# Reordering the backward pass of an SSM-gated FFN block: convolution backward first, parameter sums spread over two stages, w1/w3 gradient copies moved to ScalarE, part of w1/w3 transposed early

## The chip, the cores and the metric

The kernel runs on one core of a Trainium2 chip. The metric is the device time of one execution in microseconds (us), lower is better. Times are medians of a few executions; executions of one kernel differ by up to 1%, so runs on the same chip beside the kernel before are compared by ratios.

## The reference, cut to what matters

The forward function is a layer norm, a state-space convolution `s` (length 2048, 576 channels, 128 states), and a gate `silu(FFN(xn))` with hidden width 4608. The kernel computes the forward result and the gradients of all inputs.

```python
def _B_ref(x, w1, w3, w2):
    gate = jnp.einsum("bsd,df->bsf", x, w1)
    up = jnp.einsum("bsd,df->bsf", x, w3)
    h = _silu(gate) * up
    return jnp.einsum("bsf,fd->bsd", h, w2)

x = A_u
xn = _layernorm(x, axis=-1)
s = _A_ref(xn, A_re, A_im, B_re, B_im, C_re, C_im, log_dt, Dskip)   # FFT convolution
g = _silu(_B_ref(xn, w1, w3, w2))
return x + s * g
# reference(): this value and its vjp with grad_out, for every input
```

The backward half has four kinds of work that matter here: the FFN weight gradients (18 groups of 256 hidden columns), the backward of the convolution (four quarters of the channels), the sums for the SSM parameters (36 chunks of 16 channels, then one "final parameter step"), and the FFN input gradients (16 tiles of 128 rows).

Of the kernel before, what the change touches and what calls it, by code (L numbers as in the profile page):

```python
# [11 lines left out]
ALU = mybir.AluOpType  # L12
# [48 lines left out]
class K:  # L61
# [393 lines left out]
    def kgen_chunk(self, ch, E, lhs, SEL, mp, sb, sb1, ps, ps1):  # L455
# [27 lines left out]
        nc.gpsimd.tensor_scalar(out=pz[:, :, :, 0].rearrange("p g h d a -> p (g h) (d a)"),  # L483
# [202 lines left out]
    def ffn_hidden(self, wp, gup, ps, T0, TA):  # L686
# [4 lines left out]
        NT = 2  # L691
        nfull = D // P
# [3 lines left out]
        for fb in range(F // FB):  # L696
# [9 lines left out]
            for i0 in range(0, LT, NT):  # L706
                self.at(T0 + TA * 4 * fb + TA * 4 * i0 // LT)
                g_t = gup.tile([P, NT, FB], BF16, name="g_t")
                u_t = gup.tile([P, NT, FB], BF16, name="u_t")
                s_t = gup.tile([P, NT, FB], BF16, name="s_t")  # L710
                h_t = gup.tile([P, NT, FB], BF16, name="h_t")
                for q in range(NT):
# [8 lines left out]
                    nc.scalar.activation(out=s_t[:, q, :], in_=pg[:], func=ACT.Silu)  # L721
                    if q % 2 == 0:
                        nc.vector.tensor_copy(out=g_t[:, q, :], in_=pg[:])
                    else:
                        nc.scalar.copy(out=g_t[:, q, :], in_=pg[:])  # L725
                    nc.scalar.copy(out=u_t[:, q, :], in_=pu[:])
                nc.vector.tensor_tensor(out=h_t[:], in0=s_t[:], in1=u_t[:], op=ALU.mult)
                nc.sync.dma_start(out=self.H_dram[i0:i0 + NT, :, f0:f0 + FB].rearrange("t p f -> p t f"), in_=h_t[:])
                for k in range(FB // self.FG):
                    gs = slice(k * self.FG, (k + 1) * self.FG)  # L730
                    for (dst, src) in ((self.G_dram, g_t), (self.U_dram, u_t)):
                        nc.gpsimd.dma_start(out=dst[fb * (FB // self.FG) + k, :, i0:i0 + NT, :], in_=src[:, :, gs])  # L732
# [71 lines left out]
    def phase5_ssm_bwd(self, T0, TQ):  # L804
        nc, cfg = self.nc, self.cfg
        D, LT, N = cfg.D, cfg.LT, cfg.N
        Wq = D // 4
        with self.tc.tile_pool(name="b_fix", bufs=1) as fix, \
                self.tc.tile_pool(name="b_ps", bufs=3, space=bass.MemoryType.PSUM) as ps:
            S_all = fix.tile([P, 4, D], FP32, name="S_all")  # L810
            self.lcol = fix.tile([P, LT], FP32, name="lcol")
# [3 lines left out]
            self.ones_col = fix.tile([P, 1], BF16, name="ones_col")  # L815
            nc.vector.memset(self.ones_col[:], 1.0)
            self.dskip_row = fix.tile([P, D], BF16, name="dskip_row")
# [5 lines left out]
            for g in range(4):  # L823
                with self.tc.tile_pool(name="b_gk", bufs=1) as gkp:
                    gK = gkp.tile([P, 2, 2, LT, Wq // 2], BF16, name="gK")
                    with self.tc.tile_pool(name="b_k", bufs=1) as kp, \
                            self.tc.tile_pool(name="b_z", bufs=2) as zp:
                        self.conv_bwd_quarter(g, gK, kp, zp, ps, T0 + g * TQ, TQ * 0.45)
                    with self.tc.tile_pool(name="g_q", bufs=3) as qp:
                        self.param_quarter(g, gK, S_all, qp, ps, T0 + (g + 0.45) * TQ, TQ * 0.55)  # L830
            self.at(T0 + 4 * TQ)
            self.phase5_final(fix, S_all, ps)

    def conv_bwd_quarter(self, g, gK, kp, zp, ps, T0, TQ):
# [38 lines left out]
        for i in range(NB - 1, -1, -1):  # L873
# [21 lines left out]
            for h in range(2):  # L895
                for hf in range(2):
                    nc.sync.dma_start(out=gK[64 * h:64 * h + 64, hf, :, i * KT:(i + 1) * KT, :].rearrange(
                        "p k t d -> p k (t d)"), in_=st[64 * hf:64 * hf + 64, h].rearrange("p k t d -> p k (t d)"))
# [20 lines left out]
    def param_quarter(self, g, gK, S_all, qp, ps, T0, TQ):  # L919
# [3 lines left out]
        for cc in range(NQ):  # L923
            ch = g * NQ + cc
            self.at(T0 + TQ * cc / NQ)
# [25 lines left out]
    def phase5_final(self, big, S_all, ps2):  # L951
# [3 lines left out]
        with self.tc.tile_pool(name="gf", bufs=2) as fp, self.tc.tile_pool(name="gfo", bufs=3) as fo, \  # L955
                self.tc.tile_pool(name="gfp", bufs=1) as pp:
# [76 lines left out]
    def backward(self, T0, TG, TS, TQ):  # L1033
        nc, cfg = self.nc, self.cfg
        D, L, LT, F = cfg.D, cfg.L, cfg.LT, cfg.F
# [3 lines left out]
        with self.tc.tile_pool(name="e_w", bufs=2) as wp, \  # L1039
                self.tc.tile_pool(name="e_in", bufs=2) as inp, \  # L1040
                self.tc.tile_pool(name="e_el", bufs=2) as elp, \
                self.tc.tile_pool(name="e_gw", bufs=2) as gwp, \
                self.tc.tile_pool(name="e_ps_h", bufs=3, space=bass.MemoryType.PSUM) as ps_h, \
                self.tc.tile_pool(name="e_ps_gw", bufs=2, space=bass.MemoryType.PSUM) as ps_gw:
            self.phase5_ssm_bwd(T0 + TS, TQ)
            NG = F // self.FG
            for gi in range(NG + 1):
                self.at(T0 + TG * gi)
                if gi < NG:
                    tiles = self.phase6_elementwise(gi, wp, inp, elp, ps_h)  # L1050
                if gi > 0:
                    self.phase6_weight_grads(gi - 1, prev, self.go_o, gwp, ps_gw)
                prev = tiles

# [55 lines left out]
    def phase6_weight_grads(self, gi, tiles, go_o, gwp, ps_gw):  # L1110
# [20 lines left out]
        for (nat, oname) in ((gu_n, "out_11"), (gg_n, "out_10")):  # L1131
            for c in range(nfull):
# [5 lines left out]
                nc.vector.tensor_copy(out=gw[:], in_=pw_[:, 0:FG])  # L1138
# [8 lines left out]
        nc.vector.tensor_copy(out=gw[:], in_=pw_[:, 0:FG])  # L1147
# [3 lines left out]
    def phase6_inputs(self):  # L1151
# [4 lines left out]
        with self.tc.tile_pool(name="x_w", bufs=1) as wpool, \  # L1156
                self.tc.tile_pool(name="x_in", bufs=3) as inp, \
                self.tc.tile_pool(name="l_sb", bufs=2) as sb, self.tc.tile_pool(name="l_sm", bufs=4) as sm, \
                self.tc.tile_pool(name="x_ps", bufs=2, space=bass.MemoryType.PSUM) as ps:
            w1T = wpool.tile([P, FT, D], BF16, name="w1T")  # L1160
            w3T = wpool.tile([P, FT, D], BF16, name="w3T")
            for (do, dsz) in cfg.dch:
                for (w, wT) in (("B_w1", w1T), ("B_w3", w3T)):
                    self.nat_transpose(wT[:, :, do:do + dsz], aps[w][do:do + dsz, :])
            for i in range(cfg.LT):
                ggc = inp.tile([P, FT, P], BF16, name="ggc")
                guc = inp.tile([P, FT, P], BF16, name="guc")
                self.nat_transpose(ggc[:], self.GG_dram[i])
                self.nat_transpose(guc[:], self.GU_dram[i])
                if True:  # L1170
                    px = [ps.tile([P, 512], FP32, name=f"px{pi_}") for pi_ in range(len(pieces))]
# [4 lines left out]
                    self.dma(go_t[:], aps["grad_out"].flatten_outer_dims()[i * P:(i + 1) * P, :])  # L1176
                    for fi in range(FT):
                        for ai, (act, wT) in enumerate(((ggc, w1T), (guc, w3T))):
                            for pi_, (po, pw) in enumerate(pieces):
                                nc.tensor.matmul(px[pi_][:, 0:pw], lhsT=act[:, fi, :],  # L1180
                                                 rhs=wT[:, fi, po:po + pw], start=(fi == 0 and ai == 0),
                                                 stop=(fi == FT - 1 and ai == 1))
# [6 lines left out]
    def ln_bwd_tile(self, sb, sm, gx, i, go_t):  # L1189
# [9 lines left out]
        t2 = sb.tile([P, D], FP32, name="t27")  # L1199
# [7 lines left out]
        u = sb.tile([P, D], FP32, name="u7")  # L1207
# [11 lines left out]
def kernel(  # L1219
# [35 lines left out]
    with k.ctx:  # L1255
# [5 lines left out]
        matp = mats.enter_context(tc.tile_pool(name="mats", bufs=1))  # L1261
# [13 lines left out]
        with tc.tile_pool(name="go_keep", bufs=1) as gop:  # L1275
# [37 lines left out]
```

## The kernel before: the parts that the change touches

A scheduler fixes the order of each engine's instructions when the program is built, and in the traces of this case an engine works them off in that order; `self.at(t)` gives the following instructions a priority, it does not delay them. The FFN groups ("the weight pass") and the whole SSM backward share one stretch. The line marked L1138 empties a bank of PSUM, the memory that TensorE writes its results to.

```python
    def phase5_ssm_bwd(self, T0, TQ):                     # cut
            for g in range(4):                            # quarter by quarter:
                with self.tc.tile_pool(name="b_gk", bufs=1) as gkp:
                    gK = gkp.tile([P, 2, 2, LT, Wq // 2], BF16, name="gK")
                    ...
                        self.conv_bwd_quarter(g, gK, kp, zp, ps, T0 + g * TQ, TQ * 0.45)
                    ...
                        self.param_quarter(g, gK, S_all, qp, ps, T0 + (g + 0.45) * TQ, TQ * 0.55)
            self.phase5_final(fix, S_all, ps)             # the final parameter step

    def param_quarter(self, ...):                         # one chunk, cut
                            nc.tensor.matmul(T[h][...], lhsT=qT[hs, k, d8, :], rhs=gK[...], start=True, stop=True)
                        ...
                        nc.vector.tensor_tensor(out=pr[:], in0=T[h][...], in1=pz[...], op=ALU.mult)     # L944
                        nc.vector.tensor_reduce(out=S_all[...], in_=pr[...], op=ALU.add, axis=AX.XY)    # L947

    def phase6_elementwise(self, gi, ...):                # cut
            for j in range(2):
                nc.scalar.copy(out=gh[:, j], in_=ph[j][:])
            for (dst, t_) in ((self.GU_dram, gu), (self.GG_dram, gg)):
                nc.vector.tensor_tensor(out=pair(t_)[:, :, sl], in0=gh[:], in1=pair(t_)[:, :, sl], op=ALU.mult)
                for j in range(2):
                    nc.scalar.dma_start(out=dst[...], in_=t_[:, ts, :])

    def phase6_weight_grads(self, gi, ...):               # cut; gwp has 2 buffers, ps_gw has 2 banks
                pw_ = ps_gw.tile([P, 512], FP32, name="pgw")
                for tt in range(LT):
                    nc.tensor.matmul(pw_[:, 0:FG], lhsT=self.xn_bf[...], rhs=nat[:, tt, :], ...)        # L1135
                gw = gwp.tile([P, FG], BF16, name="gw13")
                nc.vector.tensor_copy(out=gw[:], in_=pw_[:, 0:FG])                                      # L1138
                nc.gpsimd.dma_start(out=aps[oname][...], in_=gw[:])                                     # L1139

    def phase6_inputs(self):                              # after the weight pass; x_in has 3 buffers, cut
            for (do, dsz) in cfg.dch:
                for (w, wT) in (("B_w1", w1T), ("B_w3", w3T)):
                    self.nat_transpose(wT[:, :, do:do + dsz], aps[w][do:do + dsz, :])   # ten transposes on Sync
            for i in range(cfg.LT):
                self.nat_transpose(ggc[:], self.GG_dram[i]); self.nat_transpose(guc[:], self.GU_dram[i])
                ...                                       # 144 matmuls px, then layer-norm backward
```

## Time and profile before

| stretch (us from the start) | what runs | TensorE busy | VectorE busy |
|---|---|---|---|
| 0 to 818 | SSM forward, FFN hidden | 658 | 576 |
| 834 to 1014 | FFN output | 156 of 180 | 89 |
| 1014 to 2196 | weight pass and SSM backward | 945 | 887 |
| 2196 to 2251 | transposes of w1, w3 | 0 | 0 |
| 2251 to 2547 | input gradients | 285 | 62 |

The time is 2547.58 us (median of three). In the table of instruction groups (columns: line, engine, operation, output and inputs, shapes, count; then busy us and mean ns; then idle time before it and what ended most of it) the copy of the w1/w3 gradients out of PSUM is a small thing:

```profile
L1138 DVE CAST gw<-pgw 128x256 bf16<-128x256 f32 x144 | 59.3, 421 | 121.7 <-DMA out_dram<-gw 75.2
```

It takes 0.42 us, but TensorE may wait far longer than that for it. The timeline of TensorE late in the pass (start, us, engine, line and operation; in brackets the idle time before and its releaser) shows the worst case:

```profile
2113.74 3.65 PE L1135 MATMUL pgw<-gu_n,xn_bf 128*128 128x256 bf16 x32 [1.19 <-ACT gw L1128]
2140.32 2.29 PE L1135 MATMUL pgw<-gu_n,xn_bf 128*128 128x256 bf16 x10 [22.93 <-DVE gw L1138]
```

Both banks are full after 32 matmuls. VectorE is then working through the final parameter step, some 0.2 us an instruction, and twelve products of the next group at 0.68 us; TensorE stands 22.9 us until the copy's turn comes.

### The profile page before, as it was taken

The page shows a single profiled execution, that of the slowest core. Times are in us where ns is not written, and L with a number is a line of the kernel's source. Part 1 is how long each engine was busy: PE and PEld are TensorE (multiplying, and loading weights), DVE is VectorE, ACT ScalarE, POOL GpSimd, SP SyncE. Part 2 cuts the span into 40 slices and gives each one's busy share as a digit, 9 for nine tenths or more (in the row PEclk, how much of TensorE's full clock was granted, in tenths as well). Part 3 has the DMA queues.
Part 4 walks back from the last instruction along what each step waited for, and adds up shares of the span by engine and source line. Part 5 has one row for each costly group of instructions (what it writes and reads, how often), then busy time and mean ns, then how long its engine had stood idle before and what let it go on. Part 6 is the DMA issues. An engine that isn't in the chain of part 4 may idle for free.

```text
span 2547.2 us, 42384 instructions
## 1 busy us (share of the span) xinstructions
PE 2045.9 (80%) x16790; PEld 1356.5 (53%) x16790; DVE 1615.1 (63%) x2986; ACT 846.5 (33%) x1299; POOL 607.8 (24%) x871
## 2 busy tenths in 40 slices
PE   0698888888996797878887888878788884459998
PEld 0323333333553575566665566656666552347777
DVE  6316888887975354788867886968686876002212
ACT  0355777667553112522242224322332221000000
POOL 1004887777333211211111111111111110100000
PEclk9657888888998898989899889979998886779999
DMA  3246767666757877567446644586446532599882
GB/s 77 68 182 210 236 224 236 227 223 213 241 188 170 205 189 168 168 158 157 136 118 153 144 121 129 160 153 143 127 134 168 144 103 68 132 213 167 166 179 62
DMA packets 617303, 411.40 MB, mean 162 GB/s; under 512 B 422096, under 2 KB 561488, under 8 KB 612496
## 3 DMA queue, kind: packets, MB, share of 16 engines
q1 hardware_dynamic: 477984, 232.15, 37.7%
q0 software_dynamic: 31824, 109.16, 13.8%
q10 hardware_dynamic: 107296, 67.39, 9.5%
q8 instruction: 131, 2.15, 0.4%
q14 instruction: 68, 0.56, 0.1%
HBM read 125.93 MB, written 185.65 MB: 122 GB/s over the span
## 4 chain that ended last, share of the span: by engine, by line
PE 28%; DVE 16%; issue 13%; DMA 9%; SPq 4%; ACT 3%; POOL 1%; ACTq 1%; POOLq 0%; DVEq 0%
PE px L1180 11%; PE ph L1098 4%; SPq L1056 3%; PE et_ps L937 3%; PE pgw L1124 3%; DMA out_dram<-gw 2%; DMA w2T<-w2r 2%; DVE cm_t L602 2%; PE et_ps L578 2%; PE pgw L1135 2%; DVE pr_q L944 1%; DVE gg_n L1084 1%; DVE cm_t L599 1%; PE pg L718 1%; DVE h_n L1085 1%
## 5 line engine op out<-in xcount | busy, mean ns | idle before, releaser
L1135 PEld LDWEIGHTS <-xn_bf 128*128 128x128 bf16 x2304 | 238.0, 104 | 147.3 <-issue 107.2
L1180 PE MATMUL px<-w1T,ggc 128*128 128x288 bf16 x1152 | 237.2, 288 | 54.6 <-DMA ggc<-GG_dram 54.6
L1180 PE MATMUL px<-w3T,guc 128*128 128x288 bf16 x1152 | 237.1, 288 | 3.7 <-DMA guc<-GU_dram 3.7
L1101 ACT CAST gh<-ph 128x512 bf16<-128x512 f32 x144 | 79.2, 592 | 454.6 <-PE ph L1098 178.7
L1135 PE MATMUL pgw<-gu_n,xn_bf 128*128 128x256 bf16 x1152 | 166.8, 306 | 78.1 <-DVE gw L1138 75.0
L944 DVE TENSOR_TENSOR pr_q<-et_ps,pz 128x512 f32<-128x512 f32 x288 | 185.5, 683 | 53.9 <-PE et_ps L937 52.8
L1098 PE MATMUL ph<-w2T,goT 128*128 128x256 bf16 x1152 | 190.1, 296 | 11.6 <-DMA w2T<-w2r 7.6
L718 PEld LDWEIGHTS <-xnT 128*128 128x128 bf16 x1152 | 110.6, 104 | 163.4 <-issue 79.4
L1184 DVE TENSOR_TENSOR gx<-px,gxs 128x288 f32<-128x288 f32 x32 | 13.2, 453 | 280.7 <-PE px L1180 280.7
L718 PE MATMUL pg<-wmB_w,xnT 128*128 128x512 bf16 x576 | 173.5, 421 | 13.3 <-ACT g_t L725 10.2
L947 DVE TENSOR_REDUCE S_all<-pr_q 128x8 f32<-128x512 f32 x288 | 184.2, 678 | 0.0
L732 POOL DMA_DIRECT2D G_dram<-g_t x144 | 105.7, 735 | 327.2 <-DVE q_k L473 160.5
L1139 POOL DMA_DIRECT2D out_dram<-gw x144 | 77.5, 540 | 429.0 <-DVE gw L1138 408.4
L718 PE MATMUL pu<-wmB_w,xnT 128*128 128x512 bf16 x576 | 172.3, 411 | 0.1
L937 PE MATMUL et_ps<-gK,qT 64*128 64x64 bf16 x1152 | 133.8, 289 | 39.7 <-DMA GU_dram<-gu_n 15.1
L772 PE MATMUL po<-w2g,hc 128*128 128x288 bf16 x1152 | 147.8, 290 | 17.0 <-DMA w2g<-in_B_w_dram 17.0
L1124 PE MATMUL pgw<-go_o,h_n 128*128 128x288 bf16 x1152 | 159.6, 288 | 1.6 <-DVE gw L1147 0.7
L1180 PEld LDWEIGHTS <-ggc 128*128 128x128 bf16 x1152 | 113.2, 98 | 83.9 <-issue 54.9
L1098 PEld LDWEIGHTS <-goT 128*128 128x128 bf16 x1152 | 101.9, 103 | 94.3 <-issue 55.9
L1135 PE MATMUL pgw<-gg_n,xn_bf 128*128 128x256 bf16 x1152 | 133.2, 276 | 20.2 <-DVE gw L1138 20.2
L772 PEld LDWEIGHTS <-hc 128*128 128x128 bf16 x1152 | 113.0, 99 | 48.5 <-issue 17.7
L1138 DVE CAST gw<-pgw 128x256 bf16<-128x256 f32 x144 | 59.3, 421 | 121.7 <-DMA out_dram<-gw 75.2
(309 smaller groups left out, 4206.0 us busy)
## 6 DMA issues: line engine op xcount, KB each, us to landing
Q_dram<-q_k SPq DMA_DIRECT2D x36, 512.0 KB, 4.5
G_dram<-g_t POOLq DMA_DIRECT2D x144, 128.0 KB, 3.8
U_dram<-u_t POOLq DMA_DIRECT2D x144, 128.0 KB, 3.8
H_dram<-h_t SPq DMA_DIRECT2D x72, 256.0 KB, 4.3
gg_n<-G_dram POOLq DMA_DIRECT2D x18, 1024.0 KB, 5.5
h_n<-U_dram POOLq DMA_DIRECT2D x18, 1024.0 KB, 5.8
GU_dram<-gu_n ACTq DMA_DIRECT2D x144, 128.0 KB, 2.0
GG_dram<-gg_n ACTq DMA_DIRECT2D x144, 128.0 KB, 2.5
```

The lines of the kernel that those rows point to most:

```text
L718: nc.tensor.matmul(pt[:], lhsT=xnT[:, c, ts], rhs=wm[w][:, c, :], start=(c == 0), stop=False)
L732: nc.gpsimd.dma_start(out=dst[fb * (FB // self.FG) + k, :, i0:i0 + NT, :], in_=src[:, :, gs])
L772: nc.tensor.matmul(po_[:, pi_, 0:pw], lhsT=hc[:, fi, :], rhs=w2[fi][:, po:po + pw], start=(fi == 0), stop=(fi == FT - 1))
L937: nc.tensor.matmul(T[h][:, 1 - k, dd].rearrange("p k (f t) -> p k f t", f=2), lhsT=qT[hs, k, d8, :], rhs=gK[hs, :, :, :, cc * 8 + d8].rear ...
L944: nc.vector.tensor_tensor(out=pr[:], in0=T[h][:].rearrange("p r d k a -> p (r d) k a"), in1=pz[:, dg, h, s:s + 2].rearrange("p r d a -> p ...
L947: nc.vector.tensor_reduce(out=S_all[:, 2 * s:2 * s + 2, d0:d0 + 4].rearrange("p k d -> p d k"), in_=pr[:].rearrange("p (r d) k a -> p d k ...
L1098: nc.tensor.matmul(ph[j][:, k, :].rearrange("p (a f) -> p a f", f=P), lhsT=lw, rhs=rh, start=(n == 0), stop=(n == nfull))
L1101: nc.scalar.copy(out=gh[:, j], in_=ph[j][:])
L1124: nc.tensor.matmul(pgw[pi_][:, 0:pw], lhsT=hn[:, tt, fl * P:(fl + 1) * P], rhs=go_o[:, tt, po:po + pw], start=(tt == 0), stop=(tt == LT - 1))
L1135: nc.tensor.matmul(pw_[:, 0:FG], lhsT=self.xn_bf[:, tt, c * P:(c + 1) * P], rhs=nat[:, tt, :], start=(tt == 0), stop=(tt == LT - 1))
L1139: nc.gpsimd.dma_start(out=aps[oname][c * P:(c + 1) * P, fb:fb + FG], in_=gw[:])
L1180: nc.tensor.matmul(px[pi_][:, 0:pw], lhsT=act[:, fi, :], rhs=wT[:, fi, po:po + pw], start=(fi == 0 and ai == 0), stop=(fi == FT - 1 and ai ...
```

## The change

Its intent: balance. The convolution backward of all four quarters goes first; its result gK is put to DRAM and read back for each quarter of parameter chunks; these are paced so that about a quarter of them, with the final step, lands in the input-gradient stage, where VectorE was idle. The w1/w3 gradient copies go from VectorE to ScalarE. A third of w1/w3 (12 of 36 row blocks) is transposed early, the rest after the pass. To make room, x_in gets two buffers and some tiles shrink. In the FFN hidden stage a negation goes from GpSimd to VectorE and 288 stores become 144.

```diff
 # FFN hidden stage
-        nc.gpsimd.tensor_scalar(out=pz[:, :, :, 0]..., scalar1=-1.0, ...)
+        nc.vector.tensor_scalar(out=pz[:, :, :, 0]..., scalar1=-1.0, ...)
-                for k in range(FB // self.FG):
-                    gs = slice(k * self.FG, (k + 1) * self.FG)
-                    for (dst, src) in ((self.G_dram, g_t), (self.U_dram, u_t)):
-                        nc.gpsimd.dma_start(out=dst[fb * (FB // self.FG) + k, :, i0:i0 + NT, :], in_=src[:, :, gs])
+                for (dst, src) in ((self.G_dram, g_t), (self.U_dram, u_t)):
+                    nc.gpsimd.dma_start(out=dst[fb * ng:(fb + 1) * ng, :, i0:i0 + NT, :]..., in_=src[:]...)
 # backward: order and pools
-            self.phase5_ssm_bwd(T0 + TS, TQ)
+            self.ssm_bwd_conv(T0, TQ, ps)                # all four quarters; gK goes to gK_dram
+            wA = out.enter_context(pool(name="x_wA", bufs=1, side="right"))
+            self.at(T2 - 150)
+            wT = [self.load_wT(wA, 0, FA)]               # FA = 12 row blocks of w1 and w3
+            self.ssm_bwd_params(T1, TC, S_all, ps)       # TC = 16: pace of the chunks; gK loaded per quarter
+            self.phase5_final(out, fix, S_all, ps)
 # weight gradients
-                nc.vector.tensor_copy(out=gw[:], in_=pw_[:, 0:FG])
+                nc.scalar.copy(out=gw[:], in_=pw_[:, 0:FG])
 # input gradients
-                self.tc.tile_pool(name="x_in", bufs=3) as inp, \
+                self.tc.tile_pool(name="x_in", bufs=2) as inp, \
+                    if i == 0:
+                        wT = wT + [self.load_wT(wB, FA, FT)]
-                    self.dma(go_t[:], aps["grad_out"]...)
+                    nc.scalar.dma_start(out=go_t[:], in_=aps["grad_out"]...)
```

(Cut: side="right" of pools, layouts of g_t, u_t, s_t, bf16 of one temporary, the pool of the chunks' tiles from three buffers to two, the pace of the FFN groups from 40 to 36, and the index arithmetic.)

## The prediction

> **What bounds the kernel now.** I read the page's 40 slices first, then the busy times by stage, then who waits for whom inside the longest stage, then the chain of waits. The slices show that no engine is full all the way:
>
> ```profile
> PE   0698888888996797878887888878788884459998
> DVE  6316888887975354788867886968686876002212
> PEclk9657888888998898989899889979998886779999
> ```
>
> TensorE and VectorE are both at 7 to 8 tenths through the middle, then VectorE falls to nearly nothing while TensorE runs full; between them lies a dip of both. By stage (columns: busy us of TensorE, its weight load, VectorE, ScalarE, GpSimd, each with its count; then granted clock, DMA share, GB/s):
>
> ```profile
> 215.00:625.00 410.00, 348.62 (x3326) 148.81 (x3327) 344.56 (x490) 294.97 (x384) 319.63 (x369) 0.86 0.69 225
> 625.00:818.00 193.00, 178.96 (x1231) 95.98 (x1229) 150.24 (x185) 98.86 (x214) 76.51 (x106) 0.98 0.69 200
> ...
> 1014.00:2200.00 1186.00, 945.31 (x8244) 716.36 (x8244) 887.22 (x1860) 335.77 (x551) 169.78 (x318) 0.88 0.53 136
> 2200.00:2251.00 51.00, 0.00 (x0) 0.00 (x0) 0.00 (x0) 0.00 (x0) 0.00 (x0) 0.50 1.08 229
> 2251.00:2547.00 296.00, 285.25 (x2304) 226.39 (x2304) 62.38 (x128) 12.42 (x32) 0.00 (x0) 0.98 0.78 153
> ```
>
> The weight pass (18 groups of the FFN backward plus the whole SSM backward) takes 1186 us with VectorE busy 887 and TensorE 945. Then 51 us with every engine idle: the transposes of w1 and w3. Then 296 us of input gradients, with TensorE full and VectorE idle four fifths. Inside the weight pass:
>
> ```profile
> PE pgw L1135 <- DVE gw L1138: 95.3, 22, 22.9
> PE ph L1098 <- ACT gh L1101: 35.9, 18, 12.7
> PE pgw L1142 <- DVE gw L1138: 15.7, 7, 4.6
> ```
>
> ```profile
> DVE gw L1138 <- DMA out_dram<-gw: 75.2, 35, 5.8
> DVE pr_q L944 <- PE et_ps L937: 52.8, 37, 11.9
> ```
>
> TensorE waits 111 us for VectorE to empty the weight-gradient banks, while VectorE either works through parameter sums queued ahead of that copy or stands at it, as its output buffer is still being stored. So the pass has two engines near their limit that take turns, and one in-order queue, VectorE's, in which small urgent copies stand behind long work.
>
> **What the Trainium skill says.** Perfetto Trace Analysis, Optimization Strategy: where the most-contended engine changes over time, interleaving the regimes may help. The trace agrees that there is something to interleave: VectorE 75% busy in one stage, 21% in the last. TensorE: Matmul & The Clock Gate, the table of what matters for kernels: no TensorE gaps over about 3 us, or the clock falls back. The trace agrees: 0.88 granted in the gappy pass, 0.98 in the full stage. GPSIMD Engine Reference, Key points: GpSimd shares its SBUF interfaces with VectorE, contending with two-input VectorE instructions. The trace agrees; the same 128x512 product beside GpSimd copies and without:
>
> ```profile
> 414.40 0.86 DVE L493 TENSOR_TENSOR v_k<-t_k 128x512 bf16<-128x512 bf16 x1
> ...
> 424.59 0.41 DVE L493 TENSOR_TENSOR v_k<-t_k 128x512 bf16<-128x512 bf16 x1
> ```
>
> DMA: Bandwidth & Descriptors, DMA Transpose: the plain one is issued from Sync or Scalar only. Here all go through Sync, one after the other:
>
> ```profile
> 2196.52 4.81 SPq L1056 DMA_TRANSPOSE w1T<-in_B_w_dram  x1
> ...
> 2239.99 2.93 SPq L1056 DMA_TRANSPOSE w3T<-in_B_w_dram  x1
> 2243.28 4.76 SPq L1056 DMA_TRANSPOSE ggc<-GG_dram  x1
> 2248.09 4.92 SPq L1056 DMA_TRANSPOSE guc<-GU_dram  x1
> ```
>
> **The change part by part.** Matmul and VectorE work stay the same in amount; what moves is their order. I counted the changed program's TensorE order, cut at each group's end. Convolution backward: groups 0 to 6. Of the 1152 parameter matmuls (32 to a chunk, 36 chunks), 128 lie in group 7, 64 to 88 in each of groups 8 to 16, 28 before the end of group 17, about 330 (ten chunks) in the first ten of 16 input-gradient tiles, then the final parameter step. Before, a group held 128 parameter matmuls or some 200 of the convolution.
>
> Costs at full clock. A group's weight gradients alone: 25.5 us (the last group, 2171.0 to 2196.5, has nothing beside). Its 80 ph matmuls: 17 in 2.06 us in the timeline, so 9.5 us. Together 35. Parameter matmuls: eight in 1.05 us, 24 in 2.0, so about 0.1 us each. Convolution: 62 ns apart. VectorE: two products take 1.19 us, likewise two reductions; a chunk has eight of each, so 9.5 us. Its FFN products: 16 of 0.684 us, 10.4 us a group with overlap. Convolution: its groups sum to 293 us, some 270 with overlap.
>
> (1) Groups 1 to 6, to the end of the convolution: TensorE 6 x 35 + 1328 x 0.0625 = 293 us; VectorE 245 (what group 0 leaves) + 62 = 307. Now VectorE is slightly the bound. Before, two groups and nearly one quarter of convolution (1291 to 1436, 1559 to 1695, 1820 to 1947) took 145, 136 and 126 us for a need of 95 on either engine, 70%. Without the copies on VectorE I take 77%: 400 us.
> (2) Groups 7 to 16: group 7 is bound by VectorE (4 chunks, 38 + 10.4 = 48), so 56 us. The other nine: TensorE 35 + 7.4 = 42, VectorE 2.3 x 9.5 + 10.4 = 32. TensorE is the bound; with 12% for waits 47 us each. Sum 479. Before, groups with four chunks took 62 us (1169.9 to 1231.4) against a need of 52 on VectorE.
> (3) Group 17 with 28 parameter matmuls: 29 us. Group 0 ended at 1102 before; I take 1098. End of the pass: 1098 + 400 + 479 + 29 = 2006, against 2196.
> (4) Copies of the weight gradients go to ScalarE, which was busy 336 of 1186 us; 162 x 0.42 = 68 us are added. This is already used in (1) and (2).
> (5) The transposes. A third of w1 and w3 (12 of 36 row blocks) is now loaded during the pass. After it: ggc and guc (10 us), then ten transposes of two thirds' length, 8 x 3.35 + 2 x 2.0 = 31 us. TensorE does a third of tile 0 meanwhile (6 us). Offset at the start 41 - 6 = 35 us, where it was 2196.5 to 2255.4, 59.
> (6) The input-gradient stage: 16 x 17.8 = 285 (284.5 in the chain), plus 324 x 0.125 = 41 for the parameter matmuls, which cut into full streams; VectorE, 10 x 9.5 + 62 + about 50 for the final step, is far from full. ggc and guc have two buffers instead of three: a tile's pair takes about 5 us to issue the first and 9.2 to land the second, some 15 us from a freed buffer, just inside 17.8; I add 10 us for that and for Sync standing before output stores. 35 + 285 + 41 + 10 = 371.
> (7) The tail after the last matmul stays 7.5 us.
> (8) FFN hidden stage: 36 negations of 1.58 us leave GpSimd, and 144 of 288 stores of 0.735 us; 163 of 320 us saved there. But TensorE waits there for VectorE (43 us on v_k), not for GpSimd, and VectorE gets the negations (0.35 us each, my guess) and must stand until GpSimd's four copies (3.9 us beside two-input products) have ended, since the negation stands ahead of v_k in its order. Relief from sharing and new standing I set against each other: -4 us, the 1098 of (3).
>
> Sum: 2006 + 371 + 7.5 = 2384.5; I say **2385 us**, 6.4% less.
>
> **The rivals.** (a) The pass stays as long per group as now, because the queues and not the balance decide: at 62 us a group in part (2) the end is about 140 us later, 2525. For it: after the change the in-order queues still mix FFN and SSM work, and the Sync queue still waits on ph (its largest wait). Against it: less VectorE work per group, and the copies off its queue. Full strength is unlikely; a third of it is quite possible. (b) The input-gradient stage becomes transfer-bound: its DMA share is 0.78 on average and near 0.88 in full slices, and qT, pz and gK join, with fewer buffers. At 24 us a tile in ten tiles, 20 to 30 us more. For it: the share; against it: Sync issues need 15 us of a tile's 22. (c) The early part 1 gets worse, as four quarters in a row leave VectorE no parameter work to fill the convolution's chain of load, transform, product, inverse: another 50 us. (d) The FFN hidden stage gains in earnest, up to 40 us, if GpSimd's lateness drives it, or loses 30 if VectorE stands at the negation.
>
> **Range and chances.** (a) at a third, (b) or (c) each add 30 to 50 us; (d), or a pass as dense as 90%, takes off 40 to 70. I give **2310 to 2460** for 8 in 10. Faster by over 2% means below 2497: chance 0.95; within 2%: 0.04; slower: 0.01.
>
> **What would show each step.** By stage: pass from 1014 to about 2006, clock above 0.90; groups 8 to 16 at 45 to 50 us; the waits of pgw for gw smaller than 40 us in sum; no stretch over 40 us with TensorE idle at the stage change; input-gradient tiles at about 22 us with parameters and 18 without, VectorE half busy there. Wrong if groups 8 to 16 stay above 55 us, if tiles exceed 25 us with TensorE waiting for ggc or guc, or if the stages before 818 move by more than 30 us.

## The result, and the profile after

The changed kernel takes 2406.75 us (median of four, 2389.4 to 2408.83), the kernel before 2548.2 us beside it (2544.01 to 2549.65). The ratio is 0.9432, 95% interval 0.9387 to 0.9478. Ratios here are the mean time of one kernel's fast runs over the mean of the other's fast runs of the same rounds, so they are not quite the ratio of the medians quoted. One hundredth of ratio is about 25 us.

The 40 slices of the page, after:

```profile
PE   0698888788999499789888857989899996799968
DVE  6414777767788345479969674866655772276751
PEclk9656888888899799899999977999999998899989
```

The dip of both engines late in the program has become shallower (TensorE 6 and 7 tenths in slices 34 and 35, where it had 4, 4 and 5 in 34 to 36), and VectorE's long empty end now holds work. But TensorE has a new hole in the middle (slice 24, a 5). By stage (busy us of TensorE, weight load, VectorE, ScalarE, GpSimd, each with its count; clock; DMA share; GB/s):

```profile
215.00:625.00 410.00, 335.17 (x3285) 145.87 (x3322) 298.66 (x522) 292.35 (x381) 175.38 (x238) 0.87 0.66 226
625.00:818.00 193.00, 177.11 (x1209) 95.92 (x1228) 149.84 (x187) 99.57 (x217) 40.05 (x57) 0.97 0.65 194
...
1014.00:2016.00 1002.00, 879.29 (x7920) 675.82 (x7918) 693.32 (x1293) 389.76 (x707) 166.97 (x314) 0.92 0.61 156
2016.00:2059.00 43.00, 10.68 (x64) 6.57 (x62) 4.86 (x8) 0.37 (x1) 1.29 (x3) 0.61 1.09 229
2059.00:2400.00 341.00, 316.26 (x2562) 246.36 (x2562) 180.68 (x506) 14.36 (x35) 0.00 (x0) 0.96 0.87 162
```

The pass ends 180 us earlier (2016 against 2196) at a higher clock (0.92 against 0.88). From its end to the full stream of px, the input-gradient matmuls (counted from the end of TensorE's last wait of over 3 us), it now takes 43 us, not 59, and that stream takes 341 us, not 285, with VectorE 53% busy in it: -180 - 16 + 56 = -140, the whole gain of the two profiled runs. The FFN hidden stage, 215 to 818, ends where it did (821 against 818), although GpSimd's busy time in its first part fell from 320 to 175 us. The idle stage change on Sync's queue, one transfer after the other as before but with ten shorter ones:

```profile
2016.19 4.76 SPq L1091 DMA_TRANSPOSE ggc<-GG_dram  x1
2021.00 4.79 SPq L1091 DMA_TRANSPOSE guc<-GU_dram  x1
2025.84 35.49 SPq L1091 DMA_TRANSPOSE wTB_w<-in_B_w_dram  x10
```

Who waits for whom in the pass (line, releaser; us in sum, times, longest):

```profile
PE ph L1133 <- ACT gh L1136: 44.7, 21, 26.7
PE pgw L1170 <- ACT gw L1173: 32.8, 18, 5.5
```

```profile
ACT gw L1173 <- DMA out_dram<-gw: 104.0, 35, 8.1
```

TensorE's wait for the gradient copies fell from 111 to 35 us (33 in this line and 2 at L1177). The standing at full output buffers has moved along with the copies: VectorE stood 75 us for it, now ScalarE stands 104. And one new wait is 26.7 us long. The timeline of ScalarE's queue at that place (ACTq are its transfer issues):

```profile
1430.11 19.56 ACTq L1142 DMA_DIRECT2D GU_dram<-gu_n  x2
...
1453.04 1.56 ACT L1136 CAST gh<-ph 128x512 bf16<-128x512 f32 x3 [37.40 <-DMA GU_dram<-gu_n]
```

and that of Sync:

```profile
1422.64 6.91 SPq L1091 DMA_TRANSPOSE wTB_w<-in_B_w_dram  x3
1429.72 1.21 SPq L834 DMA_DIRECT2D gK<-gK_dram  x1
```

The early w1 transposes, the load of gK (1.15 MB, 22.6 us from issue to landing), the next h_n and pz all meet between 1422 and 1450 us. The issue of one of ScalarE's stores lasts 18.96 us in the trace, the copies of ph stand behind it, and TensorE stands behind those. In this program Sync's and ScalarE's transfers share a small set of semaphores, the "completion slots", and a transfer first waits until the one that used its slot before has landed. The Trainium skill, DMA: Bandwidth & Descriptors, "Why a DMA increments its semaphore by 16 and not by 1", says why a slot is not used twice at a time: "One semaphore per in-flight slot, not one per stream." The trace agrees for the second store of the pair, and its semaphore records name the holder: the store waits for the slot of the third early w1 transpose (issued at 1426.40 us), the last of that slot's 16 increments comes at 1449.18 us, and the store starts at 1449.20; in e2, e3 and e12 it is the same transpose and the same 0.02 us. The first store's own semaphores had been reached at 1428.71 and 1429.75 us, before its issue began, so why its record lasts 18.96 us the trace does not tell.

### The profile page after: what moved, and what is told of

Read it like the earlier page. It is cut to its first block, busy times and chain, and to the rows that moved or that the text cites. A ratio compares the mean times of both kernels' runs of the same rounds, so it can differ in the third digit from the quotient of the medians.

```text
span 2407.0 us, 42210 instructions
## 1 busy us (share of the span) xinstructions
PE 2008.8 (83%) x16735; PEld 1340.2 (56%) x16790; DVE 1505.0 (63%) x2860; ACT 902.7 (38%) x1461; POOL 426.5 (18%) x691
## 3 DMA queue, kind: packets, MB, share of 16 engines
q10 hardware_dynamic: 108448, 68.57, 10.4%
## 4 chain that ended last, share of the span: by engine, by line
PE 29%; DVE 13%; issue 12%; DMA 10%; SPq 4%; ACT 4%; POOL 2%; ACTq 1%; POOLq 0%; DVEq 0%
PE px L1214 10%; SPq L1091 4%; PE ph L1133 4%; PE et_ps L578 2%; DMA out_dram<-gw 2%; PE pgw L1170 2%; PE et_ps L940 2%; DMA w2T<-w2r 2%; PE et_ps L560 2%; PE pgw L1159 2%; PE pg L719 1%; PE pu L719 1%; DVE cm_t L602 1%; DVE gg_n L1119 1%; DMA gK<-gK_dram 1%
## 5 line engine op out<-in xcount | busy, mean ns | idle before, releaser
L1214 PE MATMUL px<-wTB_w,ggc 128*128 128x288 bf16 x1152 | 243.1, 292 | 33.7 <-DVE gx L1217 11.0
L1214 PE MATMUL px<-wTB_w,guc 128*128 128x288 bf16 x1152 | 242.6, 291 | 23.2 <-DMA guc<-GU_dram 12.1
L1133 PE MATMUL ph<-w2T,goT 128*128 128x256 bf16 x1152 | 174.5, 284 | 7.2 <-DMA w2T<-w2r 6.7
L1170 PE MATMUL pgw<-gg_n,xn_bf 128*128 128x256 bf16 x1152 | 143.6, 287 | 32.9 <-ACT gw L1173 32.8
L1214 PEld LDWEIGHTS <-guc 128*128 128x128 bf16 x1152 | 114.4, 99 | 56.2 <-DMA guc<-GU_dram 13.5
L1170 PE MATMUL pgw<-gu_n,xn_bf 128*128 128x256 bf16 x1152 | 141.3, 281 | 3.9 <-ACT gw L1163 3.9
L1173 ACT CAST gw<-pgw 128x256 bf16<-128x256 f32 x144 | 51.2, 380 | 248.4 <-DMA out_dram<-gw 104.0
L1159 PEld LDWEIGHTS <-h_n 128*128 128x128 bf16 x1152 | 115.2, 103 | 40.7 <-issue 5.0
L733 POOL DMA_DIRECT2D G_dram<-g_t x72 | 52.5, 728 | 465.7 <-ACT g_t L727 226.5
L1231 ACT ACTIVATE t<-gx 128x576 f32<-128x576 f32 x16 | 10.9, 684 | 324.7 <-DVE gx L1217 299.5
```

What stands on the lines that cost most here:

```text
L733: nc.gpsimd.dma_start(out=dst[fb * ng:(fb + 1) * ng, :, i0:i0 + NT, :].rearrange("g p t f -> p g (t f)"), in_=src[:].rearrange("p g t f -> ...
L1133: nc.tensor.matmul(ph[j][:, k, :].rearrange("p (a f) -> p a f", f=P), lhsT=lw, rhs=rh, start=(n == 0), stop=(n == nfull))
L1159: nc.tensor.matmul(pgw[pi_][:, 0:pw], lhsT=hn[:, tt, fl * P:(fl + 1) * P], rhs=go_o[:, tt, po:po + pw], start=(tt == 0), stop=(tt == LT - 1))
L1170: nc.tensor.matmul(pw_[:, 0:FG], lhsT=self.xn_bf[:, tt, c * P:(c + 1) * P], rhs=nat[:, tt, :], start=(tt == 0), stop=(tt == LT - 1))
L1173: nc.scalar.copy(out=gw[:], in_=pw_[:, 0:FG])
L1214: nc.tensor.matmul(px[pi_][:, 0:pw], lhsT=act[:, fi, :], rhs=wT[part][ai][:, f, po:po + pw], start=(fi == 0 and ai == 0), stop=(fi == FT - ...
```

## The experiments

Twelve kernels were run, none of them wrong in its results. The four of e1 to e4 ran on one chip, e5 to e8 on a second, e9 to e11 on a third, e12 on the second again. The changed kernel's ratio to compare with is 0.9432.

**e1: gradient copies back on VectorE.**

```diff
-                nc.scalar.copy(out=gw[:], in_=pw_[:, 0:FG])
+                nc.vector.tensor_copy(out=gw[:], in_=pw_[:, 0:FG])
```

> The changed kernel (2407 us) with one part undone: the w1/w3 weight-gradient copies out of PSUM go back from ScalarE to VectorE. Theory A, on which the prediction's steps (1), (2) and (4) rest: these copies must not stand behind parameter sums in VectorE's in-order queue; so TensorE's waits of pgw for the gw copies go back from 33 us to 80 us or more and the kernel takes 2440 to 2490 us. Rival B: the new distribution of the parameter sums alone brings the gain, because with 2 to 3 chunks a group VectorE has room for the copies: within 15 us of 2407. Rival C: the copies were the whole gain: 2520 us or more.

Measured: 2421.08 us (2414.43 to 2425.84), ratio 0.9494, so 16 us more than the changed kernel, hardly clear of noise (interval 0.9454 to 0.9534 against 0.9387 to 0.9478). TensorE's waits for the copies in the pass are 45 us in sum, against 35 with ScalarE and the 80 of theory A. The group table has the larger part:

```profile
L1170 PE MATMUL pgw<-gg_n,xn_bf 128*128 128x256 bf16 x1152 | 143.6, 288 | 34.4 <-DVE gw L1173 34.4
```

By the total, theory A falls and rival B holds. But the total hides two opposite differences. Groups 1 to 5 and group 6, of the changed kernel and then of e1 (columns as in the stages above):

```profile
1095.60:1386.80 291.20, 260.17 (x2673) 210.25 (x2673) 237.31 (x509) 135.82 (x309) 46.23 (x86) 0.97 0.54 153
1386.80:1489.90 103.10, 60.15 (x501) 45.33 (x501) 52.79 (x103) 21.68 (x35) 12.45 (x22) 0.72 0.86 164
...
1100.30:1433.70 333.40, 273.81 (x2725) 220.50 (x2724) 275.22 (x598) 123.66 (x274) 51.94 (x91) 0.93 0.51 141
1433.70:1500.70 67.00, 48.57 (x435) 37.10 (x435) 39.05 (x77) 14.21 (x14) 9.42 (x19) 0.85 0.85 211
```

With the copies on VectorE, groups 1 to 5 take 42 us more: 333 us, and 332 in e9, against 285 to 294 in the changed kernel and the eight other runs of the new order. TensorE waits there 27 us for VectorE's convolution results (Z, ZZ, gx) in place of 5, and 17 us for the copies in place of 10. Group 6 takes 36 us less, mostly because the stall described above did not come. Groups 7 to 16 took 494 us (499 with ScalarE): there, with the sums stretched out, VectorE has time for the copies, as rival B says. Beside the convolution the copies off VectorE are worth 8 us a group; the stall in group 6 spent it.

**e2: edits of the FFN hidden stage undone** (with the old layout of the tiles; cut).

```diff
-        nc.vector.tensor_scalar(out=pz[:, :, :, 0]..., scalar1=-1.0, ...)
+        nc.gpsimd.tensor_scalar(out=pz[:, :, :, 0]..., scalar1=-1.0, ...)
-                    nc.gpsimd.dma_start(out=dst[fb * ng:(fb + 1) * ng, :, i0:i0 + NT, :]..., in_=src[:]...)      # 144
+                        nc.gpsimd.dma_start(out=dst[fb * (FB // self.FG) + k, :, i0:i0 + NT, :], in_=src[:, :, gs])  # 288
```

> The changed kernel with its edits to the FFN hidden stage undone: negation on GpSimd again, 288 stores of G and U in place of 144, tiles laid out as before. Theory A (step 8 of the prediction, and the trace after, where that stage ends at 821 us against 818 before): worth nothing, 2400 to 2415 us, the end of group 0 within 6 us of 1095.6. Rival: the edits gave up to 40 us and something else took it back: 2430 us or more.

Measured: 2402.82 us (2394.55 to 2403.63), ratio 0.9417; group 0 ends at 1095.1 against 1095.6. The edits are worth nothing that can be seen, as theory A said. The changed kernel's trace shows a reason, VectorE's wait for GpSimd's four copies ahead of the moved negation (215 to 640 us):

```profile
DVE pz_k L483 <- POOL pz_k L482: 45.9, 30, 2.3
```

VectorE's busy time from 215 to 625 us fell from 345 to 299 us, and this new standing of 45.9 us took its place; TensorE's wait for v_k stayed (58 us before, 57 after).

**e3: early load undone, first attempt.**

```diff
-            self.at(T2 - 150)
-            wT = [self.load_wT(wA, 0, FA)]
-                        wT = wT + [self.load_wT(wB, FA, FT)]
+                        wT = [self.load_wT(wA, 0, FA), self.load_wT(wB, FA, FT)]   # in the input-gradient part
```

> The changed kernel with the early load of twelve row blocks of w1 and w3 undone: all ten transposes of part A stand with part B after the weight pass. Step (5) says that the early load shortens the stage change by 16 to 25 us (before 59 us from the end of the pass to the full stream, after 43). Theory C (collision): the early load also costs: its transposes stand ahead of and beside the gK load at 1422 us, so that the gK load takes 22.6 us, a ScalarE store waits 19.6 us for its completion slot and TensorE stands 26.7 us in group 6. Then group 6, 103 us now, takes 75 to 85 here, the stage change 60 to 68, and the time is 2400 to 2415. Rival D: the group 6 stall comes from the gK load and the first parameter chunk alone: group 6 stays at 95 to 105 us and the time is 2422 to 2435.

Measured: 2405.48 us (2397.01 to 2413.2), ratio 0.9424; group 6 took 94 us, the stage change 43. A miss of the experiment: the scheduler put the transposes where they had been, as their buffer is free there and a call's place in the program is only a priority. Afterwards the built order of Sync showed the same sequence as the changed kernel. So it is in effect a repeat, and shows how well the number repeats: within 0.001 of ratio. It also shows that the stall in group 6 varies in a same order: 26.7 us, here 22.0, in e2 20.0 (and 26.8 in e5, 13.2 in e12).

**e4: early load held back to parameter chunk 8 by a data dependence.**

```diff
-            self.at(T2 - 150)
-            wT = [self.load_wT(wA, 0, FA)]
+            # called after chunk 8; each tile first gets five elements of S_all:
+            self.nc.vector.tensor_copy(out=t[0:1, 0, 0:cfg.D:P], in_=S_all[0:1, 0, ch * 8:ch * 8 + 5])
```

> The changed kernel with the early load of the twelve row blocks kept, but held back by a data dependence until parameter chunk 8 of 36 is summed (two copies of five elements on VectorE; the transposes overwrite them). The order of the other instructions stays. Theory C (collision at the start of the parameter sums): group 6 falls from 103 to 70 to 85 us and the whole to 2375 to 2392. Rival D (the stall comes from the gK load without the transposes): group 6 within 8 us of 103, whole within 8 us of 2407. Rival E (the stall moves to where the load is now, about group 9): group 6 falls, group 9 rises by as much, whole within 8 us.

Measured: 2405.83 us (2394.4 to 2412.01), ratio 0.9431. The profiled run has group 6 at 78 us in place of 103, and the store's standing fell to a third:

```profile
1429.74 5.87 ACTq L1147 DMA_DIRECT2D GU_dram<-gu_n  x2
```

TensorE's hole shrank from 26.7 to 12.0 us. As the hole varies by as much in one order, all profiles together make the case: group 6 took 89 to 105 us in the five with the early load there and the copies on ScalarE (the changed kernel, e2, e3, e5, e12) and 78 to 82 us in the four without it (e4, e7, e8, e11). So the collision is real. But the load costs where it went: groups 8 to 10 took 160 us here and 169 in e8, which has the same load, against 151 in the changed kernel. The median did not move: on time theory C fails, and rival E, the stall that moves, is close to what the runs show. What is left, against a spread of 18 us, is not visible.

**e5: all parameter chunks inside the weight pass.**

```diff
-        k.backward(700, 36, 60, 16, 18, gctx, mats)
+        k.backward(700, 36, 60, 11, 18, gctx, mats)
```

> The changed kernel with its parameter chunks paced at 11 us in place of 16, so that by the built order all 1152 parameter matmuls and the final parameter step lie in the weight pass and none in the input-gradient stage (one part undone: the stretching). Theory A, balance: the ten chunks cost the input-gradient stage 324 x 0.125 = 41 us of TensorE plus some 20 us of stalls near the final step, which go; in the pass they raise groups 7 to 16 from 49 to 55 to 58 us, VectorE being the busier engine again: whole 2415 to 2440 us. Rival B, full balance: each group goes back to about 62 us as before the change, the pass ends 110 us later or more, whole 2460 us or more. Rival F: stretching is worth nothing, TensorE is what counts in both stages: within 8 us of 2407.

Measured: 2414.26 us (2406.82 to 2426.07), ratio 0.9461, so about 7 us more. The pass ended at 2069 us in place of 2016, groups 7 to 16 averaged 54.3 us in place of 49.9, and the input-gradient stage gave most of it back. As a whole the stretching, the heart of the change's intent, is worth 7 us once the copies are on ScalarE, and the intervals overlap (0.9417 to 0.9505 against 0.9387 to 0.9478). That is less than theory A's lower end by a hair and at rival F's edge. Part of these 7 us is not balance: in e5 the final parameter step meets the stage change, and Sync issues its stores between the transposes:

```profile
2085.57 3.29 SPq L1091 DMA_TRANSPOSE wTB_w<-in_B_w_dram  x1
2088.96 4.11 SPq L81 DMA_DIRECT2D out_dram<-gout  x2
```

The full stream starts 67 us after the pass, not 43. In the profiled runs the pass is 53 us longer, the stage change 24 longer and the stream 60 shorter (282 us), 17 in sum. Without the 24 us nothing would be left of the worth of stretching; that is an estimate from these numbers, no run tested it.

**e6: the kernel before, with only the copies moved to ScalarE.**

```diff
-                nc.vector.tensor_copy(out=gw[:], in_=pw_[:, 0:FG])
+                nc.scalar.copy(out=gw[:], in_=pw_[:, 0:FG])
```

> The kernel before with one part of the change done alone: the w1/w3 gradient copies out of PSUM on ScalarE. Run e1 showed that in the changed order the copies are worth 14 us. Theory A (order and balance make the gain; the copies help a little): 2520 to 2545 us, ratio 0.988 to 0.998. Rival C (the copies matter where VectorE is the crowded engine, as it is in the order before): TensorE's wait of pgw for gw falls from 111 us to under 40 and the time to 2470 to 2510. Rival G: ScalarE's own queue, with its DMA issues, delays the copies more: 2555 us or more.

Measured: 2441.59 us (2434.9 to 2444.43), ratio 0.956, the largest surprise: two lines bring 112 us of the 145 (0.044 of 0.0568 in ratio; by the medians on its chip 109 us). It is below even rival C's range. In the waits of the pass:

```profile
PE pgw L1135 <- ACT gw L1138: 15.9, 10, 3.2
```

The wait that was 111 us is 16. Groups 1 to 15, which took 980 us before, took 879; the stage change is as long as before (55.1 us). ScalarE's copies cost 375 ns each, VectorE's 421, so it isn't the speed of the copy that counts, but which engine has it. ScalarE stands 88 us at full output buffers here, about as VectorE did. Moving the copy changes two things at once: its place behind other work in a queue, and VectorE's load, which at this line loses 59 us of copying and 75 us of standing; e10 takes the standing apart, no run separates the rest.

**e7: part A of w1/w3 truly late**, in memory that only comes free after the pass.

```diff
-            self.at(T2 - 150)
-            wT = [self.load_wT(wA, 0, FA)]
-                        wT = wT + [self.load_wT(wB, FA, FT)]
+                        wT = [self.load_wT(wB, 0, FA), self.load_wT(wB, FA, FT)]
```

> The changed kernel with part A of w1 and w3 placed in memory that comes free only after the weight pass, so that all twenty transposes stand after it (e3 was meant to do this and turned out to have the same order of instructions as the changed kernel: its repeat, in effect). Step (5): the time from the end of the pass to the full stream goes from 43 us to 59 to 68. Theory C (collision): group 6 falls from 103 us to 74 to 84 as in e4. Together 2395 to 2420 us. Rival D': the early load is worth its full 16 to 25 us and group 6 does not profit: 2422 to 2435.

Measured: 2413.65 us (2404.8 to 2417.2), ratio 0.9459. On Sync after the pass, which ended at 1989 us here:

```profile
1989.04 5.38 SPq L1090 DMA_TRANSPOSE wTB_w<-in_B_w_dram  x3
...
2009.08 45.00 SPq L1090 DMA_TRANSPOSE wTB_w<-in_B_w_dram  x17
```

The full stream starts at 2052, 63 us after the end of the pass, against 43; group 6 falls to 82 us. So the early load saves 20 us at the stage change as step (5) had it, and costs a part of that in group 6; in all it is worth about 7 us, not clear of noise (0.9425 to 0.9492 against 0.9387 to 0.9478). Both numbers are theory C's.

**e8: e4, and in addition the stores of the final parameter step and of out_1 issued by GpSimd.**

```diff
-                    self.dma(aps[oname][do:do + dsz, :], ob[v])        # alternately Sync and ScalarE
+                    nc.gpsimd.dma_start(out=aps[oname][do:do + dsz, :], in_=ob[v])
```

> e4 (early load held back to chunk 8) and in addition the stores of the final parameter step and of out_1 issued by GpSimd, which is idle then, in place of Sync, whose in-order queue they hold while ggc and guc of the next tile stand behind. Theory H (Sync stands at the gout stores): the three TensorE gaps of 23 us in sum at 2285 to 2330 us shrink below 8, and the time is 2380 to 2392. Rival (ggc and guc come late because two buffers or the transfers bound them): gaps stay within 6 us of 23 and the time within 6 us of e4's 2406.

Measured: 2403.52 us (2392.74 to 2409.08), ratio 0.9409, within the noise of e4. What it was to remove is Sync's standing at these stores in the changed kernel (L81 here):

```profile
2274.22 13.94 SPq L81 DMA_DIRECT2D out_dram<-gout  x7
...
2299.75 10.11 SPq L81 DMA_DIRECT2D out_dram<-gout  x5
```

While they issue, ggc of the tile after next waits behind them. In e8 the two gaps of TensorE for ggc and guc (7.2 and 5.4 us) are gone, but the third became longer, 16.0 us in place of 10.5. Its releaser:

```profile
PE px L1219 <- DVE gx L1222: 16.6, 2, 16.0
```

TensorE waits here for VectorE to empty the px banks, with the final parameter step in its queue. Half right, half a new case of the same thing.

**e9: e1 and e5 at once**: new order, chunks all in the pass, copies on VectorE.

```diff
-        k.backward(700, 36, 60, 16, 18, gctx, mats)
+        k.backward(700, 36, 60, 11, 18, gctx, mats)
-                nc.scalar.copy(out=gw[:], in_=pw_[:, 0:FG])
+                nc.vector.tensor_copy(out=gw[:], in_=pw_[:, 0:FG])
```

> Both e1 and e5 at once: the new order (convolution first, early load, new pools), but all parameter chunks inside the weight pass and the w1/w3 gradient copies on VectorE. Alone, moving the copies back costs 14 us and un-stretching 8 to 12. Theory S (the two parts are substitutes for one another: either takes the copies out of the crowd in VectorE's queue, as e6 suggests with 109 us for the copies alone in the old order): together they cost far more than the sum, 2470 to 2530 us, with TensorE's waits of pgw for gw above 70 us. Rival T (they are independent): 2425 to 2435 us. Rival U (the order 'convolution first' is itself the other large part): 2425 to 2450 us, waits of pgw for gw near 40.

Measured: 2493.54 us (2488.52 to 2504.79), ratio 0.9756: 83 us more than the changed kernel, where the parts alone give 16 and 7. Theory S, as predicted. The waits:

```profile
PE pgw L1170 <- DVE gw L1173: 88.2, 23, 35.1
```

35.1 us of it, and 12.0 in a second wait, lie in group 17, where the copies stand behind the final parameter step: group 17 took 81.5 us against 28.4 in e5, which has the same work in the pass but the copies on ScalarE. The rest is spread over the groups.

**e10: the kernel before with four gradient buffers in place of two**, copies on VectorE.

```diff
-                self.tc.tile_pool(name="e_gw", bufs=2) as gwp, \
+                self.tc.tile_pool(name="e_gw", bufs=4) as gwp, \
```

> The kernel before, its copies still on VectorE, with four output buffers for the weight gradients in place of two; the order of all instructions on TensorE, ScalarE and Sync is almost unchanged. It takes away what made VectorE stand at the copy (75 us for the store of the buffer before). Theory Q (the copies are late because they stand behind parameter products and reductions in VectorE's queue): 2530 to 2550 us. Theory W (VectorE standing at a full buffer was the main loss, and ScalarE has time to stand where VectorE has not): TensorE's wait of pgw for gw falls from 111 to below 60 us and the time is 2460 to 2510 us.

Measured: 2530.95 us (2515.39 to 2532.33), ratio 0.9896: 27 us.

```profile
PE pgw L1135 <- DVE gw L1138: 73.8, 12, 23.1
```

VectorE hardly stands at full buffers any more (3.3 us, 75 before), yet TensorE still waits 74 us for it (111 before), 23.1 us in one piece. Theory Q: the buffers are a quarter of the cost (27 of the 112 us that e6 brought). The other 85 us are the place in the queue and the 59 us of copying together.

**e11: a combined version**: e8, with 18 row blocks early in place of 12 and four gradient buffers.

```diff
-        FA = 12
+        FA = 18
-            gwp = ffn.enter_context(pool(name="e_gw", bufs=2))
+            gwp = ffn.enter_context(pool(name="e_gw", bufs=4))
```

> The changed kernel with what the runs speak for: early load held back to chunk 8 (e4) and enlarged from 12 to 18 row blocks, stores of the final step and out_1 by GpSimd (e8), four gradient buffers in place of two (ScalarE stands 104 us for them now; under theory W that costs little there). Sum of the parts: about 4 us from e8 by its median, 5 to 8 from the shorter stage change, 0 to 15 from the buffers: 2380 to 2398 us. If stalls only move: within 5 us of 2404.

Measured: 2376.0 us (2369.73 to 2386.97, five runs), ratio 0.9296, interval 0.9269 to 0.9323: the fastest kernel here, 7.0% under the kernel before and below the changed one.

```profile
1984.67 29.24 SPq L1096 DMA_TRANSPOSE wTB_w<-in_B_w_dram  x10
```

The pass ends at 2002. The smaller part B no longer waits for the end of the pass: its transposes start 17 us ahead of it, and the full stream starts 27 us after it (22 if a last wait of 3.8 us is not counted).

**e12: the changed kernel with four gradient buffers and nothing else**; every engine's order is the same instruction by instruction.

> The changed kernel with four gradient output buffers in place of two and nothing else; the built order is the same instruction by instruction on every engine. It tells apart what made e11 28 us faster than e8 by their ratios (0.9296 against 0.9409). Theory V (the stage change: in e11 the smaller part B fits where memory comes free earlier, its transposes start 17 us before the pass ends and the full stream starts 22 us after it, not 43): the buffers are worth 0 to 10 us, ratio 0.939 to 0.943. Rival W: ScalarE's standing of 104 us at full buffers delays the pass: 15 us or more, ratio 0.937 or less.

Measured: 2383.5 us (2373.71 to 2390.37, six runs), ratio 0.9346, interval 0.932 to 0.9372: by the ratio 22 us less than the changed kernel, from one digit. Rival W.

```profile
PE pgw L1170 <- ACT gw L1173: 11.9, 7, 5.1
```

The waits of pgw for gw fall from 33 to 12 us, ScalarE's standing at full buffers from 104 to 4, groups 7 to 16 from 499 to 484, and the stall in group 6 was 13.2 us in this run (the fastest of its six; the changed kernel's profiled run is the slowest of its four). The Trainium skill, Perfetto Trace Analysis, Optimization Strategy, describes the symptom for the engine that should be saturated: a gap that keeps repeating "can mean there isn't enough SBUF/PSUM for the next tile to be allocated". The trace agrees on the cause, 35 waits at the buffer, 104 us in sum, 8.1 at most; but they stand on ScalarE, which is busy 390 of 1002 us, and reach TensorE through it. What is left between e12 and e11 (0.005) no run splits: in the profiled runs all after the pass is 25 us shorter in e11, while its pass ends 23 us later (2002 against 1979).

The 2 by 2 of the two main parts, as ratios to the kernel before:

| | copies on VectorE | copies on ScalarE |
|---|---|---|
| old order | 1 | 0.956 (e6) |
| new order, chunks all in the pass | 0.9756 (e9) | 0.9461 (e5) |
| new order, chunks stretched | 0.9494 (e1) | 0.9432 (the change) |

## Why the prediction was right, point by point

The time was right: 2385 predicted, 2406.75 measured, inside the range and 0.9% above. That it came so close is in part luck, as step (1) shows. By its steps:

- **(1) Groups 1 to 6, 400 us: measured 394, by luck: two errors that cancel.** Groups 1 to 5 took 58 us each, not 67; group 6 took 103, with a stall of 26.7 us that no step foresaw. The reason given for the density, no copies on VectorE, holds and was sized too small: with the copies back (e1) groups 1 to 5 take 67 us each. That e1 needs 400 us for all six does not speak against it; there the stall did not come, and group 6 took 67 us.
- **(2) Groups 7 to 16, 479: measured 499.** The balance was right: TensorE bound, VectorE 29 to 37 us busy in groups 8 to 16. The mis-sized term is the 12% for waits. It left out ScalarE's standing at two full output buffers; with four (e12) the sum is 484.
- **(3)** 1098 and 29 us: measured 1095.6 and 27.4.
- **(4) The step that failed is the weight given to the copies.** The prediction saw the wait (111 us of pgw for gw, an in-order queue "in which small urgent copies stand behind long work") but booked the move as an aid to density inside (1) and (2) and the balance as the gain. e6 shows the move alone worth 112 us of 145; e1 that it is worth 16 in sum once the chunks are stretched (42 in groups 1 to 5, of which group 6 took 36 back); e9 that without either 83 us are lost. In groups 7 to 17 the two parts remove the same wait (moving the copies is worth 75 us there with the chunks in the pass, e9 against e5, and nothing with the chunks stretched, e1), so their worths do not add. Nothing in the sum needed this, as it was counted for both together.
- **(5) Stage change, 35 us of offset:** 43 us with 10.7 of TensorE work in it, so 32. e7 puts the early load's saving at 20 us.
- **(6) Input gradients, 371 with the start: measured 384.** Tiles with a chunk took 20.8 us and tiles without 17.6 to 18 (22 and 18 predicted). Two tiles took 31 and 33 us: 23 us of TensorE gaps around the final parameter step, where 10 us were allowed. Sync's stores were half of it, as predicted, and VectorE's queue the other half (e8).
- **(7)** 7 us. **(8)** -4 us: 0 within the noise (e2). The two effects that it set against each other are in the trace: 46 us of VectorE's busy time relieved, 45.9 us of new standing ahead of v_k. The negation takes VectorE 0.29 us, where 0.35 was guessed.

Its other signs held too: no stretch over 40 us without TensorE work at the stage change (the longest gap is 10.4 us), pgw's wait for gw under 40 us, the clock above 0.90 in the pass (0.92), the stages before 818 within 3 us.

Of the rivals: (a) did not come, the groups took 49.9 us, not 62. (b) did not: 20.8 us a tile, at a DMA share of 0.87. (c) did not: the convolution's groups 1 to 5, in a row, were denser than expected. (d) did not: e2. The range was used to the upper side by the buffers (22 us in e12) and by the final step.

What stays open: why the first store's issue in group 6 lasts 18.96 us, why the stall there did not come with the copies on VectorE (e1), how the worth of moving the copies divides between their place in the queue and VectorE's load, and what stretching is worth when the final step's stores do not hold up the stage change.

## What to carry to other kernels

When the tensor engine waits for a small copy out of PSUM, ask first in whose in-order queue the copy stands and what is ahead of it; moving it to another engine brought here, at two lines and alone, 112 of the 145 us of the whole change, and its worth and that of the rebalancing did not add, because in good part they remove one wait. A wait that has been moved to another engine, like the standing at a full output buffer, is not gone: look at the new engine's own waits and try one more buffer. Before an experiment is believed, compare the built order of instructions: a priority is not a delay, and an edit may change nothing. After it, compare stage by stage: a difference of 16 us in the total was 42 us lost in one stage and 36 won in the next.

## What the Trainium skill lacked or had wrong

- Perfetto Trace Analysis advises interleaving regimes (Optimization Strategy) and moving work from VectorE to ScalarE where VectorE is saturated (Optimizing Scalar/DVE Operations); it has no word on moving a short copy off a VectorE that is not saturated (75% busy in the pass) but that others wait for. Here the copy's move alone gave a ratio of 0.956; stretching the regimes, with the copies moved, another 0.003 (e5 against the change), not clear of noise.
- DMA: Bandwidth & Descriptors explains one completion semaphore for each transfer in flight, not that an issuing engine which waits for a slot holds up its compute: two ScalarE stores took 19.56 us to issue, the second waiting for the slot of a transpose from Sync, and TensorE stood 26.7 us.
- The same page has no figure for what transposes and large loads cost each other when they meet: in the trace of the changed kernel the 256-byte packets of Sync's queue took 188 ns on average from 1430 to 1445 us (median 56), the 8 KB packets of the loads beside them 2206 ns (median 316); in e4, without the early transposes, 23 ns (median 18) and 534 ns (median 309) in the same stretch.
- GPSIMD Engine Reference: the contention it describes shows (VectorE's busy time from 215 to 625 us fell from 345 to 299 us as GpSimd's fell from 320 to 175, and e2, with the old load, has 347 and 323 us), but relieving it by moving the negation was worth nothing in time (e2, ratio 0.9417). What the page lacks is the price of such a move: VectorE stood 45.9 us for GpSimd's copies ahead of the moved negation, and TensorE's wait for v_k stayed at 57 us (58 before).
